# Causal attention and a token/channel mixer on one core: the first score set of batch 0 taken in two halves of the queries, and output chunks with waits of their own

## The chip, the cores and the metric

The kernel runs on one core of a Trainium2 chip. The metric is the device time of one execution in microseconds; a lower number is better. The core has five engines that run side by side: PE (matmuls; loads of its weights are shown apart as PEld), DVE (vector), ACT (activation functions), POOL and SP. POOL and SP are used here mainly to issue DMA transfers.

## The reference

The inputs are `q`, `k` and `v` of shape (8, 8, 576, 64): batches, heads, sequence, head dimension. Attention is causal in blocks of 64. Its output is put together over heads into `x` (8, 576, 512) and goes through a mixer over tokens and then one over channels.

```
scores = q @ k.T / 8,  masked where query // 64 < key // 64
attn   = softmax(scores);   x = attn @ v           # heads side by side: 512 columns
h = relu(x.T @ w_tok1) @ w_tok2                    # 576 -> 256 -> 576 tokens
u = x + h.T
out = u + relu(u @ w_ch1) @ w_ch2                  # 512 -> 1536 -> 512 channels
```

## The kernel before

**A planner sets the order.** The kernel describes its work as some hundreds of operations (`P.add`), each with its engine or engines, an estimated cost, what it depends on, a priority `prio`, an `urgent` level, an earliest time `at`, PSUM banks that it takes and gives, and for loads a transfer time `xfer`. `Plan.run` plays these through with lags between engines and gives one order of operations; `Plan.search` draws changed priorities a given number of times, keeps the best order, and the kernel then emits its instructions in that order. So each engine has a fixed queue, in which a waiting instruction holds up all that stand behind it. A change of one cost can move instructions anywhere in the kernel.

**Loads.** For batch 0, SP loads `k` and `q` as float32 into a staging tile (`gT`) in pieces, for heads 0 to 3 (head group 0, `hg` 0) and then 4 to 7 (`load_qk`, L430). A row of a head holds 18 blocks of 64 values, so the sequence position is 18 a + k with k from 0 to 17 as the block. The pieces of blocks are (0, 9, 18), for group 0's `q` (0, 9, 14, 18). ACT (group 0) or ACT and DVE (group 1) cast each piece to bf16 into `raws` (L404 on ACT, L406 on DVE), and DVE transposes it by blocks into `turned` (L446), which holds `kT` and `qT`. For later batches POOL's transfers cast on the way (L423). `v` comes on POOL's queue for all batches (L475), as do the weights: token weights at L494, `wc1` and `wc2` at L517 and L526. At most eight of POOL's transfers are under way: each waits for the eighth one before it.

**Batch 0's attention** is written on its own (`first_attention`). Heads go in four pairs, j = 0 to 3. The keys of a head are five blocks of 128; the probabilities of a head lie in `e_sb` as 1536 columns, key block by key block, only for the queries that see it: columns 0 to 575 for block 0, 576 to 1023 for block 1, 1024 to 1535 for blocks 2 and 3; block 4 (the tail) is apart. A score set (`score_set`, L561) fills 512 columns of a head in PSUM from matmuls of 32 rows, two of which (`par`) add up, four heads side by side in the array. The two double banks `sc` hold a pair each. One exponential (L580) writes a pair's 1024 columns; the first set is made for all four heads, heads 2 and 3 in single banks (`mm`), with an exponential for each (L761). The sets are made in the order 2, 1, 0, the tail between them (`first_tail`, L713, exponentials L730). `mask` (L586) clears the corners on DVE.

`head_out` multiplies the probabilities of a head with `v` (L602) in two chunks of query blocks, (0, 1) and (2, 3); a column of ones in `v` gives the sums. DVE takes the reciprocal (L622) and multiplies (L628). `ends_out` does the last 64 queries of a pair (L658, then L680 and L686). Before, both chunks wait for all exponentials and masks of the pair and for all of `v`:

```
deps = exps + v_ready[hg] + pad
done.append(head_out(0, 4 * hg + h, deps, -2900 + j, urgent=1))
```

**Then the mixer of batch 0:** for each pair of heads, token-up (L855, L859) with a ReLU (L841), an identity matmul that adds x (L888), the product with `w2` (L903), and a copy into `uT` (L918). The channel matmuls L1078 need all of `uT`; L1390 and L1398 go down again. Later batches are interleaved with these: scores of batch 1 stand right ahead of the first L1078. Late in the kernel L1183 and L1307 do the channel mixer with fewer products.

**Fillers.** PE starts with 16 matmuls of 512 columns on zeros (`WARM`, L376), and up to 110 more of 256 columns (`KEEP`, L383) may be placed where PE has nothing else, up to a planned time of 20 us. Before holds 32 of the latter.

Of the kernel before, what the change touches and what calls it, by code (L numbers as in the profile page):

```python
# [22 lines left out]
class Op:  # L23
# [4 lines left out]
        "users", "need", "key", "waiting", "ready", "start", "end", "engine", "n", "mode", "at", "urgent", "until", "quick", "stick",  # L28
# [173 lines left out]
def kernel(  # L202
# [11 lines left out]
    nc = tc.nc  # L214
# [78 lines left out]
    WARM, KEEP = 16, 110  # L293
# [76 lines left out]
    def raise_clock():  # L370
# [7 lines left out]
        P.add("PE", WARM * 0.36, emit, pads["zeros"], -1e6, take=[(BANK, bank)], give=[bank])  # L378
# [29 lines left out]
    def load_qk(b, hg, after=[]):  # L408
# [4 lines left out]
        for n, (src, raw, dst) in enumerate(((k, kraw[i], kT[i]), (q, qraw[i], qT[i]))):  # L413
# [12 lines left out]
            edges = (0, 9, 18) if not (first and n) or hg else (0, 9, 14, 18)  # L426
            for f, (k0, k1) in enumerate(zip(edges, edges[1:])):
                if first:
                    def emit_load(o, k0=k0, k1=k1, hbm=hbm, st=st):
                        nc.sync.dma_start(out=st[:, D * k0 : D * k1], in_=hbm[:, D * k0 : D * k1])  # L430

                    ld = P.add("SP", 0.42, emit_load, (), -1e4 + n + 4 * hg, xfer=(0.1, 0.13)[hg] * (k1 - k0) - 0.47 * (hg + n + f == 0), at=0.7)

                    def emit_cast(o, k0=k0, k1=k1, raw2=raw2, st=st):
                        cast(o, raw2[:, D * k0 : D * k1], st[:, D * k0 : D * k1])

                    w = D * (k1 - k0)
                    if hg:
                        ld = P.add(EVAC, {"ACT": act_cost(w), "DVE": dve_cost(w, 1.6)}, emit_cast, [ld], prio + 0.1 * n, urgent=2)
                    else:  # L440
                        ld = P.add("ACT", act_cost(w), emit_cast, [ld], -1e4 + 2 + n, urgent=3)
                    reads(("g", hg), ld)
                    loads = [ld]

                def emit(o, raw2=raw2, dst=dst, k0=k0, k1=k1):
                    nc.vector.transpose(  # L446
                        dst[:, 0:S, :]
                        .rearrange("p s e -> p (s e)")
                        .bitcast(I32)
                        .rearrange("p (a k) -> p k a", k=NB)[:, k0:k1],  # L450
                        raw2.bitcast(I32).rearrange("p (k a) -> p k a", k=NB)[:, k0:k1],
                    )

                op = P.add("DVE", 0.02 + 32 * (k1 - k0) * 0.00185, emit, loads + T_war + after, prio + 0.1 * n, urgent=(2, 0)[b] if b < 2 else -1)
# [1092 lines left out]
```

## Time and profile before

| | |
|---|---|
| median of 4 runs | 293.13 us (293.00 to 293.49) |
| profiled execution | 293.20 us, span 290.8 us |
| busy: PE, DVE, ACT, POOL | 284.1, 229.5, 174.2, 62.2 us |
| PE clock granted | full in all 40 slices |
| first score matmul, first exponential | 8.23 us, 8.90 us |
| end of batch 0's last exponential | 21.01 us |
| first channel matmul (L1078) | 27.28 us |
| end of the last matmul | 287.3 us |

The profiled execution's own time is 2.4 us above its span: the span runs from the first to the last record, the time has what lies around it. PE's busy time counts the fillers, and the ends of matmuls are modelled and overlap, so it is not a measure of useful work. All times in the text are from the start of the span, unless they are of an execution.

### The profile page before, as it was taken

Reading aid. Unit: us, or ns where it says so; the run is one execution under the profiler, and the core shown is the slowest. Engines: PE = TensorE matmul, PEld = TensorE weight load, DVE = VectorE, ACT = ScalarE, POOL = GpSimd, SP = SyncE. Lnnn points to the kernel's source line nnn. Section 1 sums busy time; section 2 is a strip of 40 time slices with the busy share of each in tenths; the row PEclk is TensorE's granted clock in tenths of the full one; section 3 lists DMA queues with packets and bytes.
Section 4 is the critical chain, followed back from the end, with each engine's and each line's share of the span. In section 5 each row is a group of like instructions: output and inputs, shape, how many; then the busy total and the mean of one; then the engine's idle time right before and its main releaser. Section 6 shows DMA issues by size and latency. Waiting matters only on the chain.

```text
span 290.8 us, 7825 instructions
## 1 busy us (share of the span) xinstructions
PE 284.1 (98%) x3273; PEld 179.8 (62%) x3292; DVE 229.5 (79%) x529; ACT 174.2 (60%) x248; POOL 62.2 (21%) x99
## 2 busy tenths in 40 slices
PE   8999999999999999999999999999999999999995
PEld 3576445565557765456774547865446885556884
DVE  4767469879769979567997779678899978987983
ACT  5896966859677564877656787443467003867000
POOL 8774455531610170070023000000000000000000
PEclk9999999999999999999999999999999999999999
DMA  8999999998990299899329006141000821121044
GB/s 244 213 181 210 213 180 182 209 212 178 115 150 15 44 226 178 153 108 78 57 75 153 2 17 57 20 147 39 0 0 10 154 74 72 38 74 72 2 167 159
DMA packets 64835, 32.58 MB, mean 112 GB/s; under 512 B 53152, under 2 KB 55328, under 8 KB 64800
## 3 DMA queue, kind: packets, MB, share of 16 engines
q0 software_dynamic: 44032, 16.75, 49.2%
q1 hardware_dynamic: 20768, 15.34, 20.7%
q8 instruction: 25, 0.41, 0.6%
q14 instruction: 10, 0.08, 0.1%
HBM read 35.85 MB, written 9.44 MB: 156 GB/s over the span
## 4 chain that ended last, share of the span: by engine, by line
PE 88%; DMA 7%; POOL 1%; DVE 1%; ACT 1%; issue 1%; POOLq 0%; DVEq 0%
PE mm L1307 20%; PE mm L1078 15%; PE sc L561 9%; PE late L1183 7%; PE mm L1398 7%; PE mm L602 6%; PE mm L1183 5%; DMA vals<-in_v_dram 4%; PE mm L1105 4%; PE mm L855 4%; PE mm L952 4%; DMA raws<-in_q_dram 2%; PE mm L658 2%; PE late L1307 2%; PE mm L859 1%
## 5 line engine op out<-in xcount | busy, mean ns | idle before, releaser
L580 ACT ACTIVATE e_sb<-sc 128x1024 bf16<-128x1024 f32 x95 | 92.3, 1027 | 27.3 <-PE sc L561 27.0
L446 DVE STREAM_TRANSPOSE turned<-raws 128x288 int32<-128x288 int32 (+1 forms) x65 | 42.0, 699 | 7.4 <-ACT raws L404 3.1
L1078 PE MATMUL mm<-uT,wc_sb 128*128 128x512 bf16 x192 | 45.9, 381 | 0.1
L475 POOL DMA_DIRECT2D vals<-in_v_dram x45 | 36.8, 837 | 30.2 <-PE sc L561 20.3
L561 PE MATMUL sc<-turned 32*128 32x64 bf16 (+4 forms) x744 | 35.6, 281 | 0.7 <-DVE turned L446 0.5
L1078 PEld LDWEIGHTS <-wc_sb 128*128 128x128 bf16 x192 | 20.2, 115 | 19.7 <-issue 4.3
L841 ACT ACTIVATE gT<-mm 128x512 bf16<-128x512 f32 x37 | 22.2, 599 | 9.3 <-PE mm L1078 9.1
L1307 PEld LDWEIGHTS <-sums 128*128 128x128 bf16 x252 | 24.3, 98 | 4.4 <-issue 1.0
L628 DVE TENSOR_TENSOR x_sb<-mm,rinv 128x256 bf16<-128x256 f32 x63 | 25.5, 419 | 1.2
L602 PEld LDWEIGHTS <-e_sb 128*128 128x128 bf16 x640 | 22.4, 97 | 5.2 <-issue 1.8
L602 PE MATMUL mm<-vals,e_sb 128*128 128x65 bf16 x630 | 25.3, 193 | 0.0
L1307 PEld LDWEIGHTS <-gT 128*128 128x128 bf16 x240 | 22.8, 98 | 3.5 <-issue 0.6
L404 ACT COPY e_sb<-late 128x512 f32<-128x512 f32 x15 | 8.8, 586 | 25.6 <-PE late L1183 22.0
L561 PEld LDWEIGHTS <-turned 32*128 32x128 bf16 x752 | 12.6, 93 | 16.9 <-issue 13.5
L1330 DVE TENSOR_TENSOR o_sb<-mm,u_sb 128x512 f32<-128x512 f32 x23 | 15.7, 685 | 5.4 <-PE mm L1307 5.1
L1307 PE MATMUL mm<-wd_sb,sums 128*128 128x256 bf16 x150 | 18.4, 273 | 0.0
L586 DVE MEMSET e_sb<- 64x128 uint32 (+1 forms) x72 | 10.4, 153 | 8.8 <-ACT e_sb L580 5.7
L423 POOL DMA_DIRECT2D raws<-in_k_dram x14 | 7.6, 543 | 45.5 <-DVE turned L446 19.8
L622 DVE RECIPROCAL rinv<-mm 128x4 f32<-128x4 f32 x63 | 10.7, 176 | 7.8 <-PE mm L602 5.4
L967 DVE TENSOR_TENSOR u_sb<-mm,x_sb 128x512 bf16<-128x512 f32 x24 | 14.9, 680 | 2.0 <-PE mm L952 2.0
L843 DVE TENSOR_SCALAR gT<-mm 128x512 bf16<-128x512 f32 x15 | 10.3, 687 | 7.5 <-PE mm L1078 7.4
L855 PE MATMUL mm<-x_sb,w_sb 128*128 128x512 bf16 (+1 forms) x78 | 15.5, 314 | 0.3
(152 smaller groups left out, 475.4 us busy)
## 6 DMA issues: line engine op xcount, KB each, us to landing
out_dram<-o_sb SPq DMA_DIRECT2D x14, 512.0 KB, 3.2
raws<-in_k_dram POOLq DMA_DIRECT2D x14, 288.0 KB, 7.2
raws<-in_q_dram POOLq DMA_DIRECT2D x14, 288.0 KB, 7.7
vals<-in_v_dram POOLq DMA_DIRECT2D x28, 128.0 KB, 6.1
wc_sb<-in_moe_w_ch_dram POOLq DMA_DIRECT2D x8, 192.0 KB, 6.5
wc_sb<-in_moe_w_ch_dram POOLq DMA_DIRECT2D x3, 512.0 KB, 11.3
out_dram<-o_sb SPq DMA_DIRECT2D x10, 128.0 KB, 2.4
gT<-in_k_dram SPq DMA_DIRECT2D x4, 288.0 KB, 3.6
```

The lines of the kernel that those rows point to most:

```text
L446: nc.vector.transpose(dst[:, 0:S, :] .rearrange("p s e -> p (s e)") .bitcast(I32) .rearrange("p (a k) -> p k a", k=NB)[:, k0:k1], raw2.bit ...
L475: nc.gpsimd.dma_start(out=dst, in_=src)
L561: nc.tensor.matmul(out=home(n)[:, c0 : c0 + w], lhsT=kT[i][r, j0 : j0 + 128, par], rhs=qT[i][r, i0 : i0 + w, par], start=(par == 0), stop= ...
L580: nc.scalar.activation(dst, sc[SC.index(note["pool"])][:, :, 0:n], EXP, scale=scale)
L602: nc.tensor.matmul(out=u[:, I, 0:65], lhsT=e[:, h, c : c + 128], rhs=vt[:, J, head, 0:65], start=(J == 0), stop=(J == I),)
L628: nc.vector.tensor_tensor(out=xt[:, 0:4, 64 * head : 64 * head + 64], in0=u[:, :, 0:64], in1=ri[:, 0:4].to_broadcast([128, 4, 64]), op=MULT,)
L841: nc.scalar.activation(dst, src, RELU)
L855: nc.tensor.matmul(out=ps, lhsT=w1_sb[:, c, tt : tt + 255 : 2], rhs=xt[:, c, cols], start=(c == 0), stop=False)
L1078: nc.tensor.matmul(out=bank_of(bank), lhsT=wc1_sb[:, m, channels(cc)], rhs=uT[b % 2][:, :, m, :], start=(m == 0), stop=(m == NDM - 1),)
L1183: nc.tensor.matmul(out=bank_of(bank), lhsT=x(m), rhs=y[:, :, m, :], start=first and m == 0, stop=m == 1, skip_group_check=not first,)
L1307: nc.tensor.matmul(out=bank_of(bank)[:, 256 * i : 256 * i + 256], lhsT=x[:, kk, 128 * i : 128 * i + 128], rhs=y[:, kk], start=first and i ...
L1398: nc.tensor.matmul(out=ps, lhsT=gt[:, cc, c0 : c0 + 128], rhs=wc2_sb[:, cc, cols], start=(cc == 0 and not turned), stop=(cc == NDC - 1),)
```

## The change

- Group 0's `q` comes in two pieces, (0, 9, 18). The cast of its first piece is split: blocks 0 to 4 on ACT, 5 to 8 on DVE, and its transpose likewise. All transposes of group 0's `k` and those of the first `q` piece are marked `early`.
- Key block 0 is scored in two halves: `half_set` takes the queries of blocks 0 to 8 (f = 0) or 9 to 17 (f = 1), 288 columns of a head. Half 0 is made first, for all four heads, and waits for the early transposes only; half 1 is made pair by pair.
- `half_exp` turns such a half into exponentials. The results go to their places in `e_sb`, which are runs of 9 bf16 values, one in every 18. For the pair 0 and for all halves f = 1 one ACTIVATE covers two heads (576 columns), for heads 2 and 3 of half 0 one head each (288).
- Then set 1 (now 448 columns) and set 2 follow for group 0. Group 1 keeps its sets.
- Chunk (0, 1) of group 0's outputs waits only for the sets of key blocks 0 and 1 and two of `v`'s transfers (`soon`).
- Planning: 12 instead of 16 warm-up matmuls, other costs and transfer times for these loads, urgent levels of masks and transposes, 3000 draws instead of 1000.

```diff
-    WARM, KEEP = 16, 110
+    WARM, KEEP = 12, 110
...
-        P.add("PE", WARM * 0.36, emit, pads["zeros"], -1e6, take=[(BANK, bank)], give=[bank])
+        P.add("PE", WARM * 0.427, emit, pads["zeros"], -1e6, take=[(BANK, bank)], give=[bank], at=0.6)
...
-            edges = (0, 9, 18) if not (first and n) or hg else (0, 9, 14, 18)
+            edges = (0, 9, 18)
...
+                parts = ((k0, k1),)
+                if first and not hg and n == 1 and f == 0:
+                    parts = ((0, 5), (5, 9))
+                for c0, c1 in parts:
...
+                        elif len(parts) > 1:
+                            cs = P.add(("ACT", "DVE")[c0 > 0], (act_cost(w), dve_cost(w, 1.6))[c0 > 0], emit_cast, [ld], -1e4 + 2 + n, urgent=3)
...
+                    op.early = not f or not n
...
+    def half(t, f):
+
+        return t.rearrange("p (a k) -> p a k", k=NB)[:, :, 9 * f : 9 * f + 9]
+
+    def half_set(f, heads, deps, prio, notes):
...
+                    nc.tensor.matmul(
+                        out=t[:, 0 : S // 2].rearrange("p (a k) -> p a k", k=9),
+                        lhsT=kT[0][r, 0:128, par],
+                        rhs=half(qT[0][r, :, par], f),
+                        start=(par == 0),
+                        stop=(par == 1),
+                    )
...
+    def half_exp(f, heads, op, note, prio, pair):
...
+                src = sc[SC.index(note["pool"])][:, :, 0 : S // 2].rearrange("p h (a k) -> p h a k", k=9)
+                dst = e_sb[0][:, heads[0] : heads[0] + 2, 0:S].rearrange("p h (a k) -> p h a k", k=NB)
+                nc.scalar.activation(dst[:, :, :, 9 * f : 9 * f + 9], src, EXP, scale=scale)
...
-                [av] + deps, prio, take=[(BANK, bank)] if av is None else (), urgent=urgent,
+                [av] + (soon if soon and chunks[0] == 0 else deps), prio, take=[(BANK, bank)] if av is None else (),
+                urgent=urgent,
...
+            if hg == 0:
+                if f == 0:
+                    first_note = [{}, {}, {}]
+                    op0 = half_set(0, range(4), [op for op in ready[0] if op.early], prio - 0.05, list(zip((SC, BANK, BANK), first_note)))
+                    exps.append(half_exp(0, heads, op0, first_note[0], prio, True))
+                else:
+                    exps += [half_exp(0, (h,), op0, first_note[h - 1], prio, False) for h in heads]
+                note = {}
+                op = half_set(1, heads, ready[0], prio + 0.05, [(SC, note)])
+                exps.append(half_exp(1, heads, op, note, prio + 0.05, True))
+                exps.append(mask(e, 0, hs, list(exps), prio, urgent=2))
+            for n, s in enumerate((2, 1, 0) if hg else (1, 2)):
...
+                if n == 0:
+                    soon = exps + v_ready[hg][:2] + pad
...
-        for op in P.search(1000):
+        for op in P.search(3000):
```

Where the prediction speaks of a new order, it is the order of instructions that this planner emits for the changed kernel, engine by engine; it has no times.

## The prediction
> **What bounds the kernel now.** I read the page's 40 slices first: PE is at 9 almost everywhere, so after the start the time is PE's work. I asked for the engines' busy time in that stretch, from the first batch 1 scores to the last matmul.
>
> ```profile
> PE   8999999999999999999999999999999999999995
> DMA  8999999998990299899329006141000821121044
> 26.70:287.30 260.60, 259.23 (x2938) 164.34 (x2955) 211.54 (x465) 153.55 (x212) 42.37 (x59) 1.00 0.66 101
> ```
>
> In 260.60 us PE idles visibly for 1.37, and the list of its waits names only 0.3 of it (issue, no other engine). There is little here to win and something to lose. What is left is the start, about 27 us, and the tail, 3.5. At the start PE's high digit misleads: it is filled with matmuls on zeros (L376, L383) and waits hidden behind modelled ends. So I read the chain of waits there, in order of time:
>
> ```profile
> 12.29 5.22 DMA vals<-in_v_dram
> ...
> 17.80 7.05 DMA raws<-in_q_dram
> ...
> 24.86 1.81 DVE turned L446 x3
> ...
> 26.71 0.64 PE sc L561 x16
> 27.35 2.71 PE mm L1078 x12
> ```
>
> Batch 1's q lands at 24.84, three transposes follow, then batch 1's scores, then the first channel matmuls (L1078), from where PE is full. The timeline shows a second chain that ends almost together with it: batch 0's own.
>
> ```profile
> 6.62 1.41 PEld L383 LDWEIGHTS <-wd_sb 128*128 128x128 bf16 x12
> ...
> 7.16 0.67 ACT L404 CAST raws<-gT 128x576 bf16<-128x576 f32 x1 [0.21 <-DMA gT<-in_k_dram]
> ...
> 8.90 1.94 ACT L580 ACTIVATE e_sb<-sc 128x1024 bf16<-128x1024 f32 x2 [1.07 <-PE sc L561]
> ...
> 13.90 3.90 ACT L580 ACTIVATE e_sb<-sc 128x1024 bf16<-128x1024 f32 x4
> ...
> 19.01 2.00 ACT L580 ACTIVATE e_sb<-sc 128x1024 bf16<-128x1024 f32 x2
> ...
> 24.86 1.79 DVE L446 STREAM_TRANSPOSE turned<-raws 128x288 int32<-128x288 int32 x3 [0.41 <-DMA raws<-in_q_dram]
> 25.55 1.24 ACT L918 CAST uT<-mm 128x512 bf16<-128x512 f32 x2 [0.27 <-PE mm L903]
> ```
>
> ACT runs exponentials without a gap from 8.90 to 21.01. The last heads' outputs, the token matmuls and the copies into uT follow; the last copy ends at 26.79. L1078 needs all uT and stands behind the scores: it starts at 27.28. **The change touches the batch 0 chain; the batch 1 chain decides.**
>
> **What the Trainium skill says.**
> (1) "ScalarE: Activation LUTs", "What ACT_TABLE_LOAD costs": an ACTIVATE takes 186 ns + 0.833 per column, back-to-back ones overlapping by about 93. Agrees: 1024 columns would give 946 ns of pitch, and four above go from 13.90 to the next row at 17.70, 950 each.
> (2) "SBUF — State Buffer", "Door 1: The DMA port swizzle": SBUF has 16-byte lines, and an access that crosses to a new line pays. The new exponentials write runs of 9 bf16 (18 bytes). The trace of before shows no such write.
> (3) "TensorE: Matmul & The Clock Gate", "What's actually happening": the array runs at half rate until it has been busy some 3.4 us. The trace has eleven warm-up loads 0.43 us apart (1.20 to 5.45), then 0.22: a little longer.
> (4) "DMA: Bandwidth & Descriptors", "Issuing engines are not separate DMA queues": all queues share 16 engines. The slices agree: 9 through the start, whichever queue issues.
>
> **The change, part by part.**
>
> *Head start of ACT.* Before, the transposes are done at 7.57, but PE still has twelve fillers until about 8.03; the first scores come at 8.23, ACT at 8.90. After: 12 warm-up matmuls (eleven at 0.43 from 1.21, one at 0.22) end at 6.16, ten fillers of 0.109 at 7.25. The first half set needs both halves of k and the first of q. That q lands at 5.57 (issue 1.67 + 3.9). ACT casts 320 columns, DVE 256; the row for 256 on ACT is 0.40, for DVE I take 0.31 from its 576-column casts (0.45 to 0.72). DVE is free from the second k transpose at 5.74, casts to 6.05, transposes 4 and 5 blocks in 0.40 and 0.46 at most: 6.9. So PE starts at 7.25 and ends at 7.6. ACT however first casts the second q half (landed by 6.35; 0.67) and a k half of group 1, which before came at 7.10 and was cast 7.16 to 7.83. It stands ahead of the first exponential, so ACT starts at 7.85, **1.05 earlier**. SP issues one load fewer.
>
> *ACT's own work.* Group 0 before: five of 1024 (0.95) and two of 512 (0.47): 5.69. After: three of 576 (0.57), two of 288 (0.31), two of 896 (0.83), two of 1024: 5.89, **+0.20**; columns are equal. I take no price for the runs of 9. Bounds: nothing, or double per column, 2304 × 0.833 = 1.92; below nothing is excluded, as the columns stay the same.
>
> *Output chunks.* Chunks 0 and 1 of group 0 now stand ahead of later score sets in PE's order. Their fourth v transfer landed at 11.6 in before (issue 5.1 + 6.5), the fifth at 12.2 (5.9 + 6.3). PE waits there with the next score set (448 columns, head pair 1) queued behind: scores at 11.9 to 12.2, exponential at 12.35, where ACT would be free at 12.05: **+0.30**. The second chunk's wait is over by 12.5; its set is done by 13.0, ACT wants it at 13.2. ACT ends at 21.01 − 1.05 + 0.20 + 0.30 = 20.46.
>
> *Down to uT.* PE's new order from there: output edges (0.35) and 20 output matmuls (0.65) of the last pair, then token-up for one pair (two groups of 0.28), eight identity matmuls (0.51), two by w2 (0.43), token-up 0.56, w2 0.43, and twice identity 0.23 + w2 0.43: from 20.55 to about 25.4. The last copy (0.58) ends near 26.2 instead of 26.79. DVE's reciprocals and multiplies (0.18 + 0.42 for a head) fit between; the early chunks took half of them forward.
>
> *Batch 1's loads.* POOL's order changes: in both versions 18 transfers are ahead of batch 1's k and q, and they are the same transfers (ten v, four token weights, four of wc). With the engines full, q lands where it did: 24.84. I give that 0.5 either way, as issue waits for the transfer eight before it and the mix of sizes is new.
>
> *DVE's order for batch 1.* Before it was k, q, k, q halves, so one k half waited behind the late q; after it is k, k, q, q. Two transposes of 0.55 pitch and 0.70 at the end follow the landing, not three: scores at 26.17 instead of 26.71, L1078 at 26.74 instead of 27.28. The uT chain (26.2) is 0.5 ahead of it. **Gain 0.54**: of more than a microsecond that the first scores gain, half stays, and it comes from DVE's order.
>
> *The rest.* The planner now makes 3000 draws with other due times, so the order of all 8 batches is new. From the first L1078 on both orders hold 2940 matmuls, and 50 entries from dense matmuls into the tiled ones (scores, output edges). An entry costs about 0.13 afterwards (12 L1078 take 2.71 after scores, three times 4 in a plain run 3 × 0.86), so equal counts mean equal work. I take 0, bounds −0.3 (of the 1.37) and +0.8 (ACT or DVE late in a new place). Masks and reciprocals are equal in number. The last store is again 128 × 256 behind the last fold; a 128 × 512 store is now issued just before it: 0 to +0.3, I take 0.05.
>
> Sum: 293.20 for the profiled execution (span 290.8, 2.4 around it) − 0.54 + 0.05 = 292.71; that execution is 0.07 above the median, so **292.6**.
>
> **Rivals.**
> *A, as worked out*: 292.6, with 0.3 around it for DMA and order. Chance 0.42. A change below 0.2% (0.59 us) is about what a measurement of this kernel cannot tell from none; this case lies on that edge, half of it on each side.
> *B, the landing moves forward too.* POOL's issue of q then waits for an earlier v, and less is queued in its way. Then uT is next late: L1078 at 26.25, gain 1.03: 292.1. Against it: the same bytes. Chance 0.26.
> *C, the change does not reach the end.* The landing is 0.5 later or the new order gives half a microsecond back in a later batch: 293.1. Chance 0.10.
> *D, slower: the runs of 9.* If each 18-byte run is paid as line crossings, ACT is the bound of the start. At double price it ends 1.92 later; 0.54 of slack is used up, L1078 comes at 28.1 and the time is 294.0. It decides from a penalty of 0.54 + 0.54 = 1.08 us, 0.47 ns a column on top of 0.833. For it: the line rule; against: most columns of a run share a line. Chance 0.12.
> *E, slower: the new order starves PE* once, behind an exponential whose score banks are not free, 0.8 or more: 293.9. Before has 1.37 in all, so a new order sooner loses than wins. Chance 0.10.
>
> **How the numbers follow.** Faster: half of A and all of B, 0.47. Within 0.2%: half of A and C, 0.31. Slower: D and E, 0.22. The range takes in B with 0.3 below it and D's price: 291.8 to 294.0; A's own is 292.3 to 292.9.
>
> **What would show it.** First exponential at 7.85 with ACT's k cast just ahead of it; ACT rows of 576 columns at about 0.66 (186 + 480 ns) and not 1.1; a gap on ACT near 12; the last exponential's end near 20.5; q landing at 24.8, two transposes after it, scores at 26.2 and L1078 at 26.7; from there to the last matmul 260.0 as before. The prediction is wrong if the landing moves by more than 0.5, if L1078 waits for uT, or if the stretch after it differs from 260 by more than 0.5.

## The result, and the profile after

The changed kernel takes 294.8 us (median of 43 runs, 293.55 to 299.88), the kernel before beside it 293.27 (64 runs). The ratio is 1.0051, 95% interval 1.0040 to 1.0062: **slower by 1.5 us**. The profiled execution took 294.10 us with a span of 292.3; before it was 293.20 with 290.8. The spans differ by 1.5 like the medians; what lies around the span (1.8 and 2.4) varies from execution to execution, so I compare spans. The profiled execution of the changed kernel is one of its faster ones: the median span of its executions is 293.0. Some executions fall in a slower state (two of the 43, near 299.8, and the profiled one of e4 below, with 0.52 of TensorE's clock between 12 and 18 us); they do not count in the ratios, and that profile is not used.

First the page of the changed kernel, and its engines' busy time from the first batch 1 scores to the last matmul (start:end and length, then busy us of PE, PEld, DVE, ACT, POOL, the clock, the DMA share, GB/s). The DMA share adds up the times of all packets and divides by the time of 16 engines; packets overlap, so it can pass 1.

```profile
PE   8998999999999999999999999999999999999993
DMA  7999999996398069999929024131001713300035
26.98:287.90 260.92, 259.07 (x2933) 164.58 (x2955) 217.06 (x473) 147.57 (x203) 42.86 (x60) 1.00 0.70 101
```

The stretch is 0.3 longer than before (260.92 against 260.60). The last digits of the DMA row have changed more: 3 and 5 where before had 4 and 4. So the loss is at both ends. The chain of waits that the page follows back from the last instruction now runs through POOL's transfers and no longer names batch 1's q:

```profile
2.90 7.22 DMA vals<-in_v_dram
...
10.40 0.53 POOL w_sb L502
...
21.44 11.34 DMA wc_sb<-in_moe_w_ch_dram
...
33.92 9.82 DMA vals<-in_v_dram
```

It starts with the first v transfer, landing at 10.12. What happens to batch 0 and to batch 1's q is in the timeline (start, length, engine, line, operation, in brackets the idle time before and what ended it):

```profile
6.96 1.37 ACT L404 CAST raws<-gT 128x576 bf16<-128x576 f32 x2 [0.61 <-DMA gT<-in_q_dram]
...
8.24 0.73 ACT L619 ACTIVATE e_sb<-sc 128x576 bf16<-128x576 f32 x1
8.85 0.43 ACT L622 ACTIVATE e_sb<-mm 128x288 bf16<-128x288 f32 x1
...
10.40 1.45 POOL L502 DMA_DIRECT2D w_sb<-in_moe_w_tok_dram  x2 [2.04 <-DMA vals<-in_v_dram]
...
18.86 2.00 ACT L628 ACTIVATE e_sb<-sc 128x1024 bf16<-128x1024 f32 x2
...
24.81 1.90 ACT L963 CAST uT<-mm 128x512 bf16<-128x512 f32 x3
...
25.67 1.26 DVE L453 STREAM_TRANSPOSE turned<-raws 128x288 int32<-128x288 int32 x2 [0.88 <-DMA raws<-in_q_dram]
26.98 0.64 PE L569 MATMUL sc<-turned 32*128 32x320 bf16 x16 [0.91 <-DVE turned L453]
```

The first exponential comes at 8.24 instead of 8.90. But the last of batch 0 ends at 20.86 instead of 21.01, and the last copy into uT at 26.71 instead of 26.79: of 0.66 us, 0.1 is left. Batch 1's q lands at 25.6 instead of 24.84. Two transposes follow it, as forecast, and the scores are at 26.98 instead of 26.71; PE waits 0.91 us for them. The first channel matmuls start at 27.55, 0.27 later than before.

Now the end. The last fold is DVE's last addition into the output tile `o_sb`. First the changed kernel, then the kernel before, from SP's and DVE's timelines (SPq is SP's issue of a DMA):

```profile
285.38 0.47 SPq L1485 DMA_DIRECT2D out_dram<-o_sb  x1
286.41 0.35 SPq L1397 DMA_DIRECT2D out_dram<-o_sb  x1
286.82 0.47 SPq L1485 DMA_DIRECT2D out_dram<-o_sb  x1
287.39 1.52 SPq L1397 DMA_DIRECT2D out_dram<-o_sb  x3
...
287.94 0.42 DVE L1375 TENSOR_TENSOR o_sb<-late,e_sb 128x256 f32<-128x256 f32 x1 [0.23 <-PE late L1352]
```

```profile
277.50 1.15 SPq L1440 DMA_DIRECT2D out_dram<-o_sb  x2
...
286.46 1.66 SPq L1352 DMA_DIRECT2D out_dram<-o_sb  x3
...
287.34 0.42 DVE L1330 TENSOR_TENSOR o_sb<-mm,e_sb 128x256 f32<-128x256 f32 x1 [0.23 <-PE mm L1307]
```

The mixed output is the last 64 queries of two batches, taken together. The two stores of the last one (64 x 512 each) were issued at 277.50 before; now (L1485) they stand at 285.38 and 286.82, among the last stores. The last fold ends at 288.36, 0.60 later than the 287.76 of before, but the span ends 1.5 later. From last fold to end it is 3.9 us instead of 3.0. For the last store of all the profile gives, before and changed:

```profile
DMA to landing us min/median/max: 1.8/1.8/1.8
```

```profile
DMA to landing us min/median/max: 2.5/2.5/2.5
```

So the account of these two profiles is: 0.27 at the first channel matmuls, 0.33 on the way (the weight loads of the first channel matmuls wait once, 0.50 for wc_sb at 29.50), 0.9 at the end. The prediction had -0.54, 0 and +0.05.

### The profile page after: what moved, and what is told of

It is laid out like the page before. It is cut to its first block, busy times and chain, and to the rows that moved or that the text cites. A ratio compares the mean times of both kernels' runs of the same rounds, so it can differ in the third digit from the quotient of the medians.

```text
span 292.3 us, 7766 instructions
## 1 busy us (share of the span) xinstructions
PE 283.7 (97%) x3256; PEld 179.3 (61%) x3280; DVE 236.2 (81%) x539; ACT 168.2 (58%) x240; POOL 62.3 (21%) x99
## 4 chain that ended last, share of the span: by engine, by line
PE 82%; DMA 12%; POOL 3%; issue 1%; ACT 1%; DVE 0%; POOLq 0%; DVEq 0%
PE mm L1352 18%; PE mm L1123 11%; PE sc L569 7%; PE late L1228 7%; PE mm L1443 6%; DMA vals<-in_v_dram 6%; PE mm L650 6%; DMA wc_sb<-in_moe_w_ch_dram 6%; PE mm L1228 6%; PE late L1352 4%; PE mm L900 4%; PE mm L997 3%; PE mm L1150 3%; PE mm L707 2%; POOL vals L483 1%
## 5 line engine op out<-in xcount | busy, mean ns | idle before, releaser
L628 ACT ACTIVATE e_sb<-sc 128x1024 bf16<-128x1024 f32 (+1 forms) x94 | 91.1, 1021 | 31.6 <-PE sc L569 31.4
L453 DVE STREAM_TRANSPOSE turned<-raws 128x288 int32<-128x288 int32 (+1 forms) x65 | 41.9, 700 | 6.9 <-ACT raws L404 3.1
L569 PE MATMUL sc<-turned 32*128 32x64 bf16 (+4 forms) x736 | 34.8, 280 | 1.3 <-DVE turned L453 0.9
L650 PE MATMUL mm<-vals,e_sb 128*128 128x65 bf16 x640 | 25.6, 193 | 0.1
L886 ACT ACTIVATE gT<-mm 128x512 bf16<-128x512 f32 x34 | 20.3, 598 | 7.9 <-PE mm L1123 7.6
L569 PEld LDWEIGHTS <-turned 32*128 32x128 bf16 x736 | 12.6, 93 | 16.9 <-issue 13.6
L1375 DVE TENSOR_TENSOR o_sb<-mm,u_sb 128x512 f32<-128x512 f32 x21 | 14.2, 686 | 4.1 <-PE mm L1352 3.4
L1012 DVE TENSOR_TENSOR u_sb<-mm,x_sb 128x512 bf16<-128x512 f32 x21 | 13.4, 683 | 4.6 <-PE mm L997 4.5
L423 POOL DMA_DIRECT2D raws<-in_q_dram x14 | 7.6, 543 | 44.3 <-DVE e_sb L634 19.2
L1352 PE MATMUL mm<-wd_sb,sums 128*128 128x256 bf16 x138 | 16.9, 273 | 0.0
```

Source lines behind the costliest of these rows:

```text
L453: nc.vector.transpose(dst[:, 0:S, :] .rearrange("p s e -> p (s e)") .bitcast(I32) .rearrange("p (a k) -> p k a", k=NB)[:, k0:k1], raw2.bit ...
L569: nc.tensor.matmul(out=home(n)[:, c0 : c0 + w], lhsT=kT[i][r, j0 : j0 + 128, par], rhs=qT[i][r, i0 : i0 + w, par], start=(par == 0), stop= ...
L628: nc.scalar.activation(dst, sc[SC.index(note["pool"])][:, :, 0:n], EXP, scale=scale)
L650: nc.tensor.matmul(out=u[:, I, 0:65], lhsT=e[:, h, c : c + 128], rhs=vt[:, J, head, 0:65], start=(J == 0), stop=(J == I),)
L886: nc.scalar.activation(dst, src, RELU)
L1352: nc.tensor.matmul(out=bank_of(bank)[:, 256 * i : 256 * i + 256], lhsT=x[:, kk, 128 * i : 128 * i + 128], rhs=y[:, kk], start=first and i ...
```

## The experiments

The planner makes a new order for each kernel, so an edit of its input can change everything. I therefore wrote the planner's own order out as a list and replayed it; single operations can then be moved while all else stays. A word is an operation's number, its engine (P, A, D, G for POOL, S for SP) and the PSUM banks it takes. All kernels but the last four differ from the text of one of the two kernels in this line and what is shown. The replay adds lines, so a line has another number in each run: the exponentials of 1024 columns, L628 in the changed kernel, are L722 in e9, its transposes L453 are L547, its scores L569 are L663.

```diff
-        for op in P.search(3000):
+        for op in P.replay(ORDER):
```

Three readings of each profile carry the argument: the bytes moved from 12 to 18 us (rate times 6 us), the time from the issue of batch 1's first q to its landing, and the time from the last fold's end to the end of the span. The first of them, before and changed:

```profile
12.00:18.00 6.00, 6.00 (x116) 3.87 (x115) 3.86 (x23) 6.00 (x12) 5.12 (x10) 1.00 1.41 182
```

```profile
12.00:18.00 6.00, 5.76 (x109) 3.74 (x107) 4.46 (x23) 6.00 (x14) 6.00 (x10) 1.00 1.37 148
```

| kernel | ratio to before (95%) | GB/s, 12 to 18 us | q, issue to landing, us | first channel matmul, us | fold to end, us |
|---|---|---|---|---|---|
| before | 1 | 182 | 7.0 | 27.28 | 3.0 |
| changed | 1.0051 (1.0040 to 1.0062) | 148 | 8.1 | 27.55 | 3.9 |
| e1: head changed, rest before | 1.0189 (1.0154 to 1.0224) | 128 | 7.9 | 28.77 | 3.1 |
| e2: head before, rest changed | 1.0042 (1.0023 to 1.0062) | 185 | 7.5 | 27.86 | 4.3 |
| e3: changed, mixed output early | 1.0073 (1.0048 to 1.0099) | 123 | 8.6 | 29.35 | 3.0 |
| e4: changed, three loads | 1.0073 (1.0044 to 1.0102) | not used | | | |
| e5: changed, end of before | 1.0044 (1.0023 to 1.0065) | 137 | 9.2 | 28.93 | 3.1 |
| e6: before, end of changed | 1.0037 (1.0019 to 1.0054) | 185 | 7.2 | 27.41 | 5.5 |
| e7: changed, POOL order of before | 1.0041 (1.0027 to 1.0055) | 168 | 7.0 | 27.19 | 3.9 |
| e8: changed, 1000 tries | 1.0092 (1.0070 to 1.0114) | 142 | 8.4 | 28.72 | 3.1 |
| e9: e5 and e7 together | 1.0003 (0.9981 to 1.0024) | 151 | 6.9 | 27.59 | 3.1 |
| e10: e9, halves written in one piece | 1.0008 (0.9993 to 1.0024) | 155 | 7.4 | 28.14 | 3.1 |
| e11: e9, a cast moved | 1.0011 (0.9994 to 1.0029) | 156 | 7.3 | 28.23 | 3.1 |
| e12: before, 3000 tries | 1.0003 (0.9987 to 1.0020) | 169 | 6.2 | 27.40 | 3.0 |
| e25: before, plain copies | 1.0000 (0.9983 to 1.0017) | 170 | 6.6 | 27.69 | 3.0 |
| e26: e9, three loads | 0.9996 (0.9977 to 1.0014) | 187 | 6.2 | 27.48 | 2.9 |
| e27: changed, stores from ACT | 1.0068 (1.0042 to 1.0095) | 143 | 8.5 | 28.07 | 4.1 |
| e28: before, POOL order changed | 1.0071 (1.0044 to 1.0097) | 141 | 8.1 | 28.11 | 3.0 |

**One profile of a head is not enough.** Before, e2, e6 and e25 have the same order up to the first channel matmul, and it starts between 27.28 and 27.86. With the changed head it starts at 27.55 in the changed kernel's own profile, and between 28.07 and 29.35 in e1, e3, e5 and e27. So the 0.27 of the account comes from an early execution, and the head's part is probably larger. The time of q from issue to landing tells the orders apart: 6.2 to 7.5 in the nine profiles with POOL's order of before, 7.9 to 9.2 in the six with that of the changed kernel (e8 and e12 have orders of their own).

### Cutting at the first channel matmul

e1 takes the changed order up to there and then that of before; e2 is the mirror.

```diff
 e1: ORDER = changed[: first channel_up] + [op for op in before if not yet issued]
 e2: ORDER = before[: first channel_up] + [op for op in changed if not yet issued]
```

> The order of issue of the changed kernel up to the first channel_up matmul (27.55 us in its trace), and from there on the order of the kernel before, both written out as lists, with no search. Theory (two separate losses: the head is late by about 0.5 us because batch 1's q lands at 25.65 instead of 24.84, and the end is late by another 0.9 us because the planner's new draw leaves the mixed output and its stores for the last 30 matmuls): only the head's part stays, so 0.4 to 0.8 us over the kernel before, ratio 1.0015 to 1.003; the last store issued within 0.1 us of the last fold. Rival (the whole 1.5 us comes from the head, the end is only its echo): ratio 1.004 to 1.006 as in the changed kernel.

Measured: 299.1 us, ratio 1.0189 (1.0154 to 1.0224). **The cut made a wait of its own** and says nothing of either theory. DVE's timeline after the cut:

```profile
35.09 1.26 DVE L547 STREAM_TRANSPOSE turned<-raws 128x288 int32<-128x288 int32 x2 [6.95 <-DMA raws<-in_k_dram]
36.19 0.68 DVE L982 TENSOR_SCALAR gT<-mm 128x512 bf16<-128x512 f32 x1
```

In the order of before a transpose of batch 1's second k stands ahead of the relus (L982). The changed head had not issued that load yet, so DVE waited 6.95 us with the relus behind it, and PE 3.8 us for a bank.

> The mirror of the first: the kernel before up to its first channel_up matmul (27.28 us), then the order of the changed kernel. Theory of two losses: only the end's part, 0.7 to 1.1 us over the kernel before, ratio 1.0025 to 1.0035, last matmul near 287.3 and the last store issued some 0.2 us after the last fold and landing in 2.5 us. Rival (the end is an echo of the head): within 0.2 us of the kernel before, ratio 0.9993 to 1.0007.

Measured: 294.88 us, ratio 1.0042. With the head of before most of the loss is still there, and its fold-to-end time is 4.3 us. The ratio lies over the expected 1.0025 to 1.0035, but its interval takes them in; the rival's 1.0007 lies outside. The end is a loss of its own.

### The end

e3 moves the last third of the last mixed output and its two stores:

```diff
 1430P
+1431P 1432D 1433S 1434S
 1435D
```

> The changed kernel's own order written out, with one move: the last third of the last mixed output (L1443, 4 matmuls), its addition and its two 64x512 stores stand right behind the second third, some 16 us sooner, instead of among the last 30 matmuls. Theory (stores bunched behind one another on SP and in the DMA engines make the end late): 0.6 to 0.9 us less than the changed kernel, ratio to before 1.002 to 1.003, the last store issued within 0.1 us of the last fold and landing in about 1.9 us instead of 2.5. Rival (the end is set by the last matmul and a fixed landing, bunched or not): as the changed kernel, ratio 1.0045 to 1.0055.

Measured: 295.82 us, ratio 1.0073 (1.0048 to 1.0099). Half of the theory came true: fold to end is 3.0. But the time did not fall. PE's timeline shows a new wait:

```profile
274.96 1.48 PE L1446 MATMUL mm<-wd_sb,sums 128*128 128x256 bf16 x12 [0.96 <-DVE sums L1430]
```

The changed kernel's list of waits has none there: the four late matmuls had been filling a wait for DVE's sums, and taken away, 0.96 us of it is open. (The head of this profile is also 1.8 us later than the changed kernel's.) To repair the end, I therefore moved it together with the order around it. At plan time 225 us both orders have issued exactly the same operations. e5 and e6 cut there:

```diff
 e5: ORDER = changed[: at 225] + before[at 225 :]
 e6: ORDER = before[: at 225] + changed[at 225 :]
```

> The order of issue of the changed kernel up to plan time 225 us, and from there the order of the kernel before, both written out; at that point both orders have issued exactly the same operations, so no operation is moved across the cut. Theory (most of the loss is the end: mixed output last, stores bunched): the time from the last fold's end to the end of the span is 3.0 us as in the kernel before instead of 3.9, and the time is 0.7 to 1.0 us under the changed kernel, ratio to before 1.0015 to 1.003. Rival (the end is no loss of its own): 3.9 us again or a ratio of 1.0045 to 1.0055.

Measured: 294.52 us, ratio 1.0044; fold to end 3.1 as expected. The size is a miss: 0.7 to 1.0 us were expected and 0.2 came, with an interval that reaches to 0.8. Its profile has a later head again (PE waits 1.7 us for batch 1's turned q instead of 0.9). With the end repaired 1.3 us of loss are left (0.7 to 1.9), more than the 0.6 that the account has before the last fold.

> The mirror: the kernel before up to plan time 225 us, then the order of the changed kernel. Theory of the end: last fold to end of the span 3.9 to 4.3 us instead of 3.0, time 0.7 to 1.0 us over the kernel before, ratio 1.0025 to 1.0035. Rival (the loss comes from the first 30 us): 3.0 to 3.3 us, ratio 0.999 to 1.001.

Measured: 294.38 us, ratio 1.0037, 1.1 us over the kernel before with an interval from 0.6 to 1.6. From 30 us to the cut PE stands within 0.2 us of the kernel before. For the last store, this answer on L1446 gives issue and landing:

```profile
L1446 SPq DMA_DIRECT2D out_dram<-o_sb x1: 398/398/398, 288.0 to 288.0; - x1
...
DMA to landing us min/median/max: 4.3/4.3/4.3
```

Before it landed in 1.8 us, in the changed kernel in 2.5. The end of the changed order **alone** costs what was said, and here more.

e27 asks whether SP's issues or the DMA engines are the cause. It and e25, e26 and e28 leave out the 15 DMA transposes of `uT` and `umT`: plain copies stand in their place, so the channel mixing of batches 2 to 7 works on values that are not transposed. e25, the kernel before with these copies, is their base line.

```diff
-                nc.sync.dma_start_transpose(
+                nc.sync.dma_start(
...
-                        nc.sync.dma_start(
+                        (nc.scalar if b == B - 1 else nc.sync).dma_start(
                             out=out[b - 1 + kk, 512:576, :],
```

> The changed kernel's own order, but the last two 64x512 stores of the mixed output are issued by ACT, which has nothing left to do there, instead of by SP; they stay as late as they are. Plain copies in place of the DMA transposes as in the base line. Theory (SP's queue is what bunches: 0.47 us for each of these issues ahead of the last stores): last store issued within 0.1 us of the last fold, last fold to end of the span 3.0 to 3.4 us instead of 3.9. Rival (the DMA engines are what is full, 0.85 to 1.0 of their time from 287 to 290 us): 3.7 us or more again.

Measured: 295.11 us, ratio 1.0068 (1.0042 to 1.0095). The last store of L1491, and below it the engines from 287 to 291 us:

```profile
L1491 SPq DMA_DIRECT2D out_dram<-o_sb x1: 332/332/332, 288.7 to 288.7; - x1
...
DMA to landing us min/median/max: 2.8/2.8/2.8
```

```profile
287.00:291.00 4.00, 1.22 (x12) 0.85 (x9) 1.22 (x3) 0.00 (x0) 0.00 (x0) 1.00 0.93 291
```

The last store is now issued right at the last fold's end (288.68), but lands in 2.8 us, and fold to end is 4.1. **SP's issues are not the cause**: taking the two mixed stores from SP wins nothing, as the rival said. The stores themselves take longer to land. The kernel before, from 1.7 us ahead of its last fold's end like the stretch above:

```profile
286.08:290.08 4.00, 1.22 (x12) 0.84 (x9) 1.20 (x3) 0.00 (x0) 0.00 (x0) 1.00 0.66 236
```

In e27 291 GB/s move in place of 236: the DMA engines have more to store in the same four us. That they are full is not shown, as a share of 0.93 is no limit (it was 1.41 between 12 and 18 us).

### The head

e4 loads the second half of batch 0's first q in two DMAs again; e7 gives POOL's first 20 transfers the order of before.

```diff
-                        nc.sync.dma_start(out=st[:, D * k0 : D * k1], in_=hbm[:, D * k0 : D * k1])
+                        for f0, f1 in ((k0, 14), (14, k1)) if n and k0 and not hg else ((k0, k1),):
+                            nc.sync.dma_start(out=st[:, D * f0 : D * f1], in_=hbm[:, D * f0 : D * f1])
```

> The changed kernel's own order, with the second half of batch 0's first q again loaded by two DMAs, so that SP issues group 1's k and q one issue (about 0.48 us) later, as in the kernel before. Theory (group 1's loads, brought forward, hold up the first v transfer, for which POOL's ninth transfer waits): the first v transfer lands by 9.3 instead of 10.12, POOL's wait of 2.04 shrinks to 1.3 or less, batch 1's q lands at 24.9 to 25.2 instead of 25.65, the first channel_up matmul starts by 27.1 instead of 27.55, and the time falls by 0.3 to 0.6 us: ratio to before 1.003 to 1.004. Rival (POOL's own new order of transfers makes the stretch from 10 to 18 us slow, whatever SP does): q at 25.5 to 25.8, first channel_up matmul at 27.5, ratio 1.0045 to 1.0055.

Measured: 296.12 us, ratio 1.0073 (1.0044 to 1.0102). No gain is seen, and the profile can't tell more (see the first section). The question is taken up again in e26.

```diff
 e7, POOL's words in their places:
-27G 29G 31G 28G 30G  36G 164G 167G 162G 161G  34G  33G ...
+27G 31G 30G 29G 28G  33G  32G  35G 163G 162G 161G  34G ...
```

> The changed kernel's own order, but the first 20 transfers that POOL issues (all ahead of and up to batch 1's q) stand in the order of the kernel before: eight v transfers first, then w1, instead of six v, w1o and one wc1. Theory (POOL's new order makes the DMA engines run slow between 12 and 18 us): POOL's longest wait falls from 2.04 us to under 1.0, 190 GB/s or more between 12 and 14 us instead of 130, batch 1's q lands at 24.6 to 25.1 instead of 25.65, first channel_up matmul at 26.8 to 27.1, 0.3 to 0.6 us under the changed kernel, ratio 1.003 to 1.004. Rival (what is late is the first v transfer, held up by group 1's k and q, whatever comes behind it): POOL waits 1.5 us or more, q at 25.4 to 25.8, ratio 1.0045 to 1.0055.

Measured: 294.12 us, ratio 1.0041. The stretch from 12 to 18 us, and POOL's own wait:

```profile
12.00:18.00 6.00, 5.64 (x107) 3.70 (x107) 4.61 (x22) 5.91 (x13) 5.19 (x9) 1.00 1.40 168
```

```profile
POOL w_sb L596 <- DMA vals<-in_v_dram: 1.8, 1, 1.8
```

168 GB/s instead of 148; q is turned from 25.32, PE no longer waits for it, and PE runs 0.5 us ahead of the changed kernel from 30 us to its last matmul. Yet POOL still waits 1.8 us for the first v transfer, as the rival said. So in this profile the order helps, but not by way of that wait; both expectations were half right. The time alone shows no gain: 0.3 us, with some 0.5 either way, and the profiled execution is the fastest of the 18.

e9 has both repairs, that of e7 and that of e5:

```diff
 e9: ORDER = (changed with e7's words)[: at 225] + before[at 225 :]
```

> The changed kernel's order with both repairs at once: the first 20 POOL transfers in the order of the kernel before, and from plan time 225 us the order of the kernel before. Only the new start of batch 0 is then left of the change. Theory (q's landing and the end are two losses that add, and the new start itself brings nearly nothing because ACT's last exponential of batch 0 ends where it did): last fold to end of the span 3.0 to 3.2 us, no wait for batch 1's turned q, time 0.999 to 1.001 of the kernel before. Rival (something else of the change is slow too, which the two repairs do not touch): ratio 1.002 or more. Second rival (the start gains its 0.5 us once the losses are gone): ratio 0.997 to 0.9985.

Measured: 293.57 us, ratio 1.0003. **The whole loss is gone** (to within 0.6 us), and no gain stands in its place: the theory's case. PE's list of waits shows q as a small item and no other of the batch 1 chain:

```profile
PE mm L470 <- DVE wd_sb L443: 1.2, 1, 1.2
PE sc L663 <- ACT e_sb L722: 0.4, 2, 0.3
PE mm L744 <- DMA vals<-in_v_dram: 0.3, 1, 0.3
PE sc L663 <- DVE turned L547: 0.3, 1, 0.3
```

By the ratios either repair alone brought 0.2 to 0.3 us and both together 1.4; the intervals, some 0.5 us each way, allow equal parts of 0.7 at their edges. Seen from the other side, the changed head alone costs 1.3 us (e5), the changed end alone 1.1 (e6), and both together 1.5 and not 2.4. So both parts are needed for the repair, but their sizes do not add up to a settled account.

e26 is e9 with e4's two lines; e28 is the kernel before with the first 20 transfers of POOL in the order of the changed one (both with plain copies):

```diff
 e28, POOL's words in their places (numbers of the changed kernel; in the kernel before they are one higher):
-27G 31G 30G 29G 28G  33G  32G  35G 163G 162G 161G  34G ...
+27G 29G 31G 28G 30G  36G 164G 167G 162G 161G  34G  33G ...
```

> The run with both repairs (POOL's first 20 transfers and the end as in the kernel before), and the second half of batch 0's first q loaded by two DMAs again, so that SP issues group 1's k and q as late as the kernel before; plain copies in place of the DMA transposes as in the base line. Theory (group 1's loads, one issue earlier, hold up the first v transfer, and POOL waits for it): POOL's wait at its ninth transfer is under 1.0 us instead of 2.21, 1.0 MB or more is moved between 12 and 18 us instead of 0.90, PE waits 0.1 us or less for batch 1's turned q instead of 0.3, ratio within 0.0015 of the base line's or under it. Rival (the bytes are the same and the first v transfer waits for them in either order): POOL's wait 1.7 us or more, 0.95 MB or less.

Measured: 293.00 us, ratio 0.9996, base line (e25) 293.01 and 1.0000. In order e25, e26, e28, each from its own table of stretches:

```profile
12.00:18.00 6.00, 6.00 (x116) 3.79 (x115) 4.39 (x24) 6.00 (x12) 4.69 (x8) 1.00 1.38 170
```

```profile
12.00:18.00 6.00, 5.77 (x105) 3.54 (x102) 4.54 (x20) 6.00 (x13) 5.39 (x9) 1.00 1.60 187
```

```profile
12.00:18.00 6.00, 6.00 (x115) 3.78 (x115) 3.63 (x22) 6.00 (x12) 5.56 (x10) 1.00 1.36 141
```

In e26 POOL's ninth transfer no longer waits for the first (the two behind it wait 0.56 and 1.43 us), 1.12 MB move instead of e9's 0.91, and PE does not wait for batch 1's q at all. So SP's early loads do hold up the v transfer: the first one takes 5.8 us to land here, 5.6 in the kernel before, and 7.2 to 7.9 in the changed kernel, e7 and e9. In the time this makes no difference that can be told (0.9996 against 1.0003). But e28, which has SP's old loads and only POOL's new order, is slow as well:

> A base line for the three runs beside it: the kernel before, its order written out, with the 15 DMA transposes of uT and umT (batches 2 to 7) replaced by plain DMA copies of the same bytes between the same tiles; the channel mixing of these batches so works on values that are not transposed, and nothing else is left out. The first of these copies comes after 50 us and is waited for by nothing in the first 30 us or the last 20. Both theories: head and end as in the kernel before (batch 1's q waited for 0.5 us or less, last fold to end of the span 3.0 to 3.2 us), ratio 0.997 to 1.003.

Measured: 293.01 us, ratio 1.0000, fold to end 3.0. One part is a miss: PE waits 1.2 us for batch 1's q in this profile, not 0.5 or less, with the order of the kernel before.

> The kernel before with one part of the change alone: the first 20 transfers of POOL stand in the order of the changed kernel (six v, w1o, one wc1, then w1 and the other v); SP's loads and all else are as before, plain copies in place of the DMA transposes as in the base line. Theory (this order alone moves less between 12 and 18 us): 0.95 MB or less between 12 and 18 us instead of 1.10, batch 1's q turned by 26.9 or later, first channel_up matmul 0.2 to 0.6 us later than in the base line, ratio 0.001 to 0.003 over the base line's. Rival (the order hurts only together with group 1's early loads): 1.05 MB or more, ratio within 0.001 of the base line's.

Measured: 294.93 us, ratio 1.0071, against 1.0000 of the base line. Its chain of waits:

```profile
17.60 8.07 DMA raws<-in_q_dram
...
25.69 1.81 DVE turned L540 x3
...
27.54 0.64 PE sc L655 x16
```

0.85 MB move from 12 to 18 us, and q takes 8.07 us to land, as in the changed kernel (8.1), with the kernel before all around it. The first channel matmul is at 28.11 against 27.69 in the base line. The new order also makes batch 0 late: PE waits 0.8 us for a v transfer, ACT's last exponential of batch 0 ends at 21.61 instead of 20.79, and uT is ready at 27.43 instead of 26.56. **POOL's new order alone makes q late.** SP's earlier loads alone lower the rate (151 to 168 GB/s in e7, e9, e10 and e11, where e26 has 187), but not beyond the spread in when q lands: it takes 6.9 to 7.4 us there, and 6.6 to 7.5 with the order of before. The time of e28 is over the expected 0.3 to 0.9 us, with six runs and an interval down to 1.3 us; its profiled execution is the fastest of the six, 1.3 us under their median, so its profile does not show where the rest is lost.

### The start of batch 0

e10 writes the halves' exponentials next to one another, on top of e9:

```diff
-                src = sc[SC.index(note["pool"])][:, :, 0 : S // 2].rearrange("p h (a k) -> p h a k", k=9)
-                dst = e_sb[0][:, heads[0] : heads[0] + 2, 0:S].rearrange("p h (a k) -> p h a k", k=NB)
-                nc.scalar.activation(dst[:, :, :, 9 * f : 9 * f + 9], src, EXP, scale=scale)
+                src = sc[SC.index(note["pool"])][:, :, 0 : S // 2]
+                dst = e_sb[0][:, heads[0] : heads[0] + 2, S // 2 * f : S // 2 * (f + 1)]
+                nc.scalar.activation(dst, src, EXP, scale=scale)
...
-                src = bank_of(note)[:, 0 : S // 2].rearrange("p (a k) -> p a k", k=9)
-                nc.scalar.activation(half(e_sb[0][:, heads[0], 0:S], f), src, EXP, scale=scale)
+                dst = e_sb[0][:, heads[0], S // 2 * f : S // 2 * (f + 1)]
+                nc.scalar.activation(dst, bank_of(note)[:, 0 : S // 2], EXP, scale=scale)
```

> As the run with both repairs, but each half's exponentials are written next to one another (288 columns in a row) instead of in runs of 9; the columns of batch 0's first set then stand in another order, all else is the same. Theory (runs of 9 cost a part of ACT's 0.5 us of added own work): the pitch of a pair's half falls from 0.61 us to 0.53 to 0.56, of a single half from 0.31 to 0.27 to 0.29, together 0.2 to 0.3 us sooner at the last exponential, and up to 0.3 us in the time. Rival (runs cost nothing, the pieces do): pitches within 0.02 us of 0.61 and 0.31, time the same within 0.1%.

Measured: 293.81 us, ratio 1.0008 (0.9993 to 1.0024). ACT's rows, first of e9, then of e10:

```profile
8.65 0.73 ACT L713 ACTIVATE e_sb<-sc 128x576 bf16<-128x576 f32 x1
9.25 0.44 ACT L716 ACTIVATE e_sb<-mm 128x288 bf16<-128x288 f32 x1
...
13.39 1.90 ACT L722 ACTIVATE e_sb<-sc 128x896 bf16<-128x896 f32 x2 [0.23 <-PE sc L663]
```

```profile
8.71 0.64 ACT L713 ACTIVATE e_sb<-sc 128x576 bf16<-128x576 f32 x1
9.25 0.40 ACT L716 ACTIVATE e_sb<-mm 128x288 bf16<-128x288 f32 x1
...
13.35 1.90 ACT L722 ACTIVATE e_sb<-sc 128x896 bf16<-128x896 f32 x2 [0.29 <-PE sc L663]
```

A pair's half takes 0.73 in runs of 9 and 0.64 in one piece; its pitch falls from 0.60 to 0.54. Three pairs make about 0.2 us. It does not reach the last exponential (21.53 and 21.50): ACT then waits a little longer for PE's scores.

e11 moves ACT's cast of group 1's first k half behind the exponentials of the first half for all four heads (three instructions), on top of e9:

```diff
-16A 181A 207A 183A 206A        (ACT)      -17D 19D 20D        (DVE)
+181A 207A 206A 16A 183A        (ACT)      +19D 20D 17D        (DVE)
```

> As the run with both repairs, but ACT's cast of group 1's first k half, which stands ahead of the first exponential and waits for its load (0.60 us in one trace), stands behind the four exponentials of the first half; DVE's transpose of that half is moved behind the next one. Theory (that cast delays all of ACT): first exponential at 8.0 to 8.1 instead of 8.2 to 8.6, ACT's last exponential of batch 0 earlier by 0.3 to 0.6 us, the first channel_up matmul earlier by as much, ratio 0.997 to 0.999. Rival (the first half's exponentials run out of scores, since the second half's scores come at 8.9): the gap moves to 9.2, the last exponential within 0.15 us of the run with both repairs, same time within 0.1%.

Measured: 293.66 us, ratio 1.0011 (0.9994 to 1.0029). No gain.

```profile
6.80 0.46 ACT L498 CAST raws<-gT 128x320 bf16<-128x320 f32 x1 [1.73 <-DMA gT<-in_q_dram]
...
8.45 0.74 ACT L713 ACTIVATE e_sb<-sc 128x576 bf16<-128x576 f32 x1 [0.24 <-PE mm L695]
```

In this execution the first q landed at 6.8, 0.9 us after the changed kernel's, so the expected 8.0 could not come; and ACT waits for PE's scores ahead of the first exponential. Whether the cast costs anything with an earlier q is open.

### The draws

e8 and e12 change the number of tries alone (the orders that come out are written out):

```diff
 e8, of the changed kernel:   -P.search(3000)   +P.search(1000)
 e12, of the kernel before:   -P.search(1000)   +P.search(3000)
```

> The changed kernel with the planner's tries set back from 3000 to 1000, its order written out. It is another draw: the mixed output stands 18 matmul groups before the end again and its stores are planned at 275.9 and 276.4. Theory (the end of the changed kernel is the luck of its draw): last fold to end of the span 3.0 to 3.3 us; with the head's 0.5 us lost again, ratio 1.001 to 1.003. Rival (the change itself, not the draw, makes it late): ratio 1.0045 to 1.0055.

Measured: 295.85 us, ratio 1.0092. Fold to end is 3.1 us, as the theory had it: the late mixed stores belong to the draw with 3000 tries, not to the split of the score set. But this draw has a wait in another place and a late head, so the time is a miss:

```profile
63.22 0.48 PE L744 MATMUL mm<-vals,e_sb 128*128 128x65 bf16 x10 [1.88 <-DVE e_sb L728]
```

> The kernel before with the planner's tries raised from 1000 to 3000 and nothing else of the change. In the planner's own clock it ends at 289.28 instead of 289.99 (and the changed kernel with 3000 tries at 289.48). Theory (a draw that the planner rates better is a lottery on the chip, as the two draws of the changed kernel showed, which rate 0.4 us apart and run 1.2 us apart the same way): anywhere from 0.997 to 1.008, with a new wait of 0.4 us or more somewhere on PE or a span end over 3.3 us after the last fold. Rival (more tries are a gain of 0.7 us, as planned): ratio 0.9965 to 0.9985.

Measured: 293.63 us, ratio 1.0003; the gain of 0.7 us that the planner counts is not there. The planner's own ends for before, e12 and changed are 289.99, 289.28 and 289.48, and for e8 0.4 above changed; the chip's medians in the same order are 293.3, 293.6, 294.8 and 295.9. The planner's ranking does not order these four.

## Why the prediction was wrong

**Right.** *The change touches the batch 0 chain; the batch 1 chain decides*: it did. DVE's new order k, k, q, q was worth what was worked out: the scores came 1.3 us after the landing (forecast 1.33), where with three transposes behind it they would have come 0.5 later. The runs of 9 were no rival D: about 0.2 us of ACT's time (e10), not 1.9, and nothing at the end. The Trainium skill ("SBUF — State Buffer", "Door 1: The DMA port swizzle") says that an access which crosses to a new 16-byte line pays; here pieces of 18 bytes cost 0.09 us on 0.64. Whether the lines cost this, or the pattern of many short runs itself, e10 does not tell apart. The steady part kept its work: 0.3 us longer, inside the stated 0.5.

**Wrong, first: "With the engines full, q lands where it did: 24.84."** It landed at 25.6, though issued 0.3 us earlier. The argument was that the same 18 transfers stand ahead. The set was the same, its order was not: q took 8.1 us from issue to landing in place of 7.0, and 148 GB/s moved from 12 to 18 us in place of 182. e28 shows that POOL's order alone does this; e7 and e9 that the old order takes it back. SP's missing issue delays the first v transfer (e26), with no effect on the time that could be told. The prediction noted both changes ("SP issues one load fewer", "the mix of sizes is new") and gave them half a microsecond either way; they needed 0.8, all of it late.

**Wrong, second: the last store, "0 to +0.3, I take 0.05".** It was 0.9. I compared only the last two issues. The two mixed stores, 8 us earlier in the old order, had moved among the last, and the last store took 2.5 us to land instead of 1.8. e27 shows that SP's issues are not why. e2, e6, e7 and e27 have the same late stores and 3.9 to 5.5 us from fold to end; all kernels with the early ones have 2.9 to 3.1. In the time the end alone costs 1.1 us (e6).

**Wrong, third: ACT's gain.** "ACT ends at 20.46"; it ended at 20.86. The start came at 8.24 and not 7.85, as the second half of q landed at 6.9 instead of "by 6.35". ACT's own work grew by 0.5, not 0.20: with no gap in its timeline it ran 12.62 us against 12.11, and e10 puts about 0.2 of that on the runs of 9, for which no price was taken. The +0.30 for early output chunks did not come: there is no gap near 12. uT was ready at 26.7, not 26.2. And with q and the end repaired (e9, e26) even the rest of the head start is gone: uT is ready at 27.4 and 27.6 there, later than the 26.8 of the kernel before, and the first channel matmul comes at 27.6 and 27.5. Why batch 0 is later there than in the changed kernel was not taken apart.

Rival C ("the landing is 0.5 later") named the late landing at a chance of 0.10, as one that only cancels the gain; the end was in no rival. The time, 294.8, lies above all of them.

## What to carry to other kernels

When a planner is asked to plan again, read the whole new order at both ends, each DMA queue included: what stands in the last stores, and what order the first transfers have, not only which. Equal sets of transfers are not equal landings. To tell a change from a redraw, write the order out and move single parts; cut where both orders have issued the same operations, since a cut elsewhere can make waits of its own. And read a head in several profiles before a few tenths of a microsecond are put down to it.

## What was not expected of the hardware

The share of the DMA engines hardly differs between the stretch with the lower rate and the one with the higher: 1.37 with 148 GB/s in the changed kernel, 1.41 with 182 before. So the packets took about the same time and carried fewer bytes. The packet records of the two traces show which packets these were. From 12 to 18 us there are 1607 packets of v and 51 of wc in the changed kernel, and 1063 and 216 before. A packet of v has 128 bytes (a row of 64 values, as bf16) and takes 33 or 34 ns; a packet of wc has 1536 bytes and takes 142 to 159 ns. So v moves 4 bytes in a nanosecond and wc about 10, and v stood in the stretch because POOL issued four of its ten transfers after 9 us instead of two. This agrees with the Trainium skill ("DMA: Bandwidth & Descriptors", "Specifications"), which asks for 512 bytes or more for the full rate. It accounts for the lower rate. That it is also what makes q late is not shown: no run changed v's transfers alone, and between 6 and 12 us the share falls as well, from 1.67 to 1.54.

A 128 x 256 store takes 1.8 us to land in the kernel before and about 2.5 to 4.3 where the two 64 x 512 stores stand close ahead.
